# Attention and MLP in one kernel: weights cast in GpSimd's DMAs, two chunks of q, k, v asked for ahead of them, V copies ahead of loads, spare PSUM banks in the ramp

## The chip, the cores and the metric

One core of one Trainium2 chip. The metric is the device time of one execution in microseconds (us). Times are medians of a kernel's runs, all of them fast ones except where it is said (a run counts as slow when it is over 1.5% above the fastest of its kernel); "the profile" is one profiled execution. PE is TensorE, ACT is ScalarE, DVE is VectorE, POOL is GpSimd, SP is SyncE. Most DMAs of this kernel are issued from SP's queue (SPq).

## The reference, cut to what matters

```python
# q, k, v: (4, 8, 768, 64) fp32; heads 0, 2, 6 see all earlier keys ("retrieval"),
# the others see the first 4 keys (sinks) and a window of 64 ("stream")
scores = q @ k.T / 8, masked;  a = softmax(scores);  attn = a @ v
x = attn as (3072, 512)
h = x @ w_in                       # 512 x 2048
return maximum(0.01 * h, h) @ w_out   # 2048 x 512
```

## The kernel before

It works in 8 chunks of 384 tokens, two to a batch element. Per chunk it loads q, k, v (nine DMAs of 256 KB in rows of 256 B), casts them to bf16, transposes q and k on PE ("preparation"), runs attention, then the in-projection (16 steps of 4 matmuls) and the out-projection (3 tiles of 16 matmuls). From chunk 2 on these are interleaved; chunks 0 and 1 are the ramp.

`va` holds V. `vb` holds V shifted by 64 tokens and `vs` the sink rows; both are made from `va` by DMAs on SP's queue, "the V copies". They are wanted by the first stream head of an attention. Other names in the profile's lines: `kb` and `qb` are the bf16 casts of k and q, `kt` and `qt` their transposes, `ksink` the sink keys, `at` and `ats` the softmax weights, `po` and `xs` the output of attention, `pt` the PSUM tile of transposes, `psS` that of scores, `ph` and `py` those of the in- and the out-projection.

```python
def load_w(which, i):                     # 1 MB of fp32 weights into a staging tile
    t = rot.tile([128, 4, 512], FP32, name="wf", tag="wf", bufs=2)
    nc.sync.dma_start(out=t[:], in_=src)
# ... cast_w then casts it to bf16 with two copies on DVE and two on GpSimd

def cast_chunk(n):
    # ... cast k and q (chunk 0: DVE and ACT; else GpSimd)
    for g in range(3):
        nc.gpsimd.tensor_copy(va[i][:, 3 * c + g, :, 0:D], src[:, g])
    # ... V copies: vs (5 DMAs, first chunk of a batch element) and vb (2 DMAs), nc.sync

load(0, "kqv"); load_w("in", 0); load_w("in", 1)
cast_chunk(0)
for f in prep_slots(0) + attention_slots(0): f()
# ... 16 in-projection steps of chunk 0, with load(1) and weight loads and casts between them
load(2, "kqv")
cast_chunk(1)                             # its V copies stand behind load(2) on SP's queue
for f in prep_slots(1) + attention_slots(1): f()
# ... 16 in-projection steps of chunk 1
load(3, "kqv"); cast_chunk(2)
merge(out_slots(0), prep_slots(2) + attention_slots(2))
for n in range(2, NCH):
    load(n + 2, "kqv"); cast_chunk(n + 1)    # where they exist
    merge(weave(in_slots(n), out_slots(n - 1)), prep_slots(n + 1) + attention_slots(n + 1))
for f in out_slots(NCH - 1): f()
```

The softmax here doesn't subtract the row's maximum and nothing guards it: scores larger than these inputs give would overflow.

## Time and profile before

| | before |
|---|---|
| time, median (runs before the prediction) | 321.59 us |
| span of the profile | 319.7 us |
| ramp: start of the first out-projection matmul | 96.5 us |
| from there to the end of the span | 223.2 us |
| PE waiting for vb | 17.2 us in 5 waits |

The ramp's end is read off the time line of PE: the first matmul of the tile `py`. It cuts the span into a part where PE has holes and a part where PE is the bound. In a line of waits the three numbers are total us, how often, and the longest. In a time line they are start and length, then engine, line and operation, and in brackets how long the engine had stood idle and what ended it. The lines themselves are in the prediction.

### The profile page before, as it was taken

What the parts mean: (1) busy time and instruction counts of PE and PEld (TensorE: products, weight loads), DVE (VectorE), ACT (ScalarE), POOL (GpSimd) and SP (SyncE); (2) the same over time, 40 slices, a digit from 0 to 9 for tenths busy, and PEclk for the clock granted to TensorE, in tenths of its full rate; (3) what the DMA queues carried; (4) which work ended last, traced back from release to release, by engine and by line L of the source; (5) the groups of instructions that cost most, each with busy time, mean ns of one, the idle gap of its engine ahead of it and who ended that gap; (6) DMA issues with size and microseconds to landing.
All of it is one profiled execution on the core that took longest, in us unless ns stands there. A gap on an engine that the chain in (4) does not pass through costs nothing.

```text
span 319.7 us, 5340 instructions
## 1 busy us (share of the span) xinstructions
PE 257.2 (80%) x2107; PEld 149.8 (47%) x2136; DVE 119.4 (37%) x323; ACT 137.7 (43%) x296; POOL 60.5 (19%) x123
## 2 busy tenths in 40 slices
PE   0476974617897888999987989899969899999984
PEld 0244532315453444566554645565536456654431
DVE  4555524104325655243532453335334423311011
ACT  2144550507361442766262526673535357643300
POOL 6340254100074602400060024000510000000000
PEclk9996796758599999999997999999999999999999
DMA  9940799970399109900982089006920200000011
GB/s 172 282 137 3 254 229 318 221 146 1 136 281 156 57 35 202 209 35 2 194 141 69 30 172 232 10 35 138 192 67 35 83 36 20 16 35 33 33 66 66
DMA packets 84024, 36.56 MB, mean 114 GB/s; under 512 B 75808, under 2 KB 75808, under 8 KB 84000
## 3 DMA queue, kind: packets, MB, share of 16 engines
q1 hardware_dynamic: 84000, 36.24, 51.1%
q8 instruction: 16, 0.26, 0.4%
q14 instruction: 8, 0.07, 0.1%
HBM read 27.26 MB, written 6.29 MB: 105 GB/s over the span
## 4 chain that ended last, share of the span: by engine, by line
PE 47%; DMA 16%; DVE 13%; SPq 12%; issue 4%; POOL 4%; ACT 2%; POOLq 0%; ACTq 0%
PE py L364 18%; PE ph L350 11%; SPq L67 11%; DMA vb<-va 6%; PE po L198 5%; DMA qf<-in_q_dram 5%; DMA vf<-in_v_dram 4%; PE pt L165 3%; DVE kt L171 3%; DVE o L368 3%; PE psS L234 3%; PE pt L303 2%; DVE xs L297 2%; PE psS L269 2%; DMA wf<-in_moe_w_out_dram 2%
## 5 line engine op out<-in xcount | busy, mean ns | idle before, releaser
L350 PE MATMUL ph<-xt,w_in_bf 128*128 128x384 bf16 x512 | 106.0, 339 | 0.1
L364 PE MATMUL py<-w_out_bf,g 128*128 128x512 bf16 x355 | 97.0, 381 | 4.0 <-DVE o L368 2.3
L352 ACT ACTIVATE g<-ph 128x384 bf16<-128x384 f32 x128 | 63.0, 492 | 82.9 <-PE ph L350 82.4
L350 PEld LDWEIGHTS <-w_in_bf 128*128 128x128 bf16 x512 | 48.0, 101 | 33.5 <-issue 7.7
L239 ACT ACTIVATE at<-psS 128x384 bf16<-128x384 f32 x84 | 40.5, 492 | 23.0 <-PE psS L234 22.3
L364 PEld LDWEIGHTS <-g 128*128 128x128 bf16 x384 | 33.6, 98 | 27.7 <-issue 5.3
L243 DVE TENSOR_TENSOR at<-at,m_caus 128x128 bf16<-128x128 bf16 x72 | 17.4, 270 | 47.6 <-ACT at L239 47.6
L368 DVE COPY o<-py 128x512 f32<-128x512 f32 x24 | 16.6, 691 | 47.1 <-PE py L364 46.9
L171 DVE COPY kt<-pt 64x384 bf16<-64x384 bf16 x64 | 22.7, 355 | 20.4 <-PE pt L165 19.8
L234 PE MATMUL psS<-qt,kt 128*128 128x384 bf16 (+2 forms) x108 | 29.4, 315 | 0.8 <-ACT at_sink L214 0.4
L198 PE MATMUL po<-vb,ats 128*128 128x65 bf16 x100 | 11.9, 199 | 17.6 <-DMA vb<-va 17.2
L198 PE MATMUL po<-va,at 128*128 128x65 bf16 x252 | 23.5, 203 | 0.8 <-DVE at L243 0.6
L165 PE MATMUL pt<-ident,qb 128*128 128x128 bf16 x96 | 12.2, 239 | 14.4 <-DVE kt L171 11.0
L198 PEld LDWEIGHTS <-ats 128*128 128x128 bf16 x240 | 12.1, 102 | 22.8 <-issue 11.3
L304 ACT ACTIVATE xt<-pt 128x384 bf16<-128x384 bf16 x32 | 15.7, 490 | 15.9 <-PE pt L303 15.6
L165 PE MATMUL pt<-ident,kb 128*128 128x128 bf16 x96 | 12.0, 233 | 12.5 <-DVE kb L137 9.0
L198 PEld LDWEIGHTS <-at 128*128 128x128 bf16 x252 | 17.4, 104 | 8.0 <-DVE at L243 2.5
L278 DVE TENSOR_TENSOR ats<-ats,m_win 128x384 bf16<-128x384 bf16 x40 | 14.9, 372 | 16.3 <-ACT ats L274 16.1
L274 ACT ACTIVATE ats<-psS 128x384 bf16<-128x384 f32 x40 | 19.2, 490 | 3.9 <-PE psS L269 3.7
L141 POOL CAST kb<-kf 128x512 bf16<-128x512 f32 x21 | 12.4, 614 | 40.1 <-DMA kf<-in_k_dram 39.9
L297 DVE TENSOR_TENSOR xs<-po,linv 128x384 bf16<-128x384 f32 x32 | 17.8, 558 | 1.1
L165 PEld LDWEIGHTS <-qb 128*128 128x128 bf16 x96 | 6.4, 103 | 24.8 <-DVE kt L171 14.8
(45 smaller groups left out, 196.8 us busy)
## 6 DMA issues: line engine op xcount, KB each, us to landing
kf<-in_k_dram SPq DMA_DIRECT2D x24, 256.0 KB
qf<-in_q_dram SPq DMA_DIRECT2D x24, 256.0 KB
vf<-in_v_dram SPq DMA_DIRECT2D x24, 256.0 KB
out_dram<-o SPq DMA_DIRECT2D x24, 256.0 KB
wf<-in_moe_w_in_dram SPq DMA_DIRECT2D x4, 1024.0 KB
wf<-in_moe_w_out_dram SPq DMA_DIRECT2D x4, 1024.0 KB
vb<-va SPq DMA_DIRECT2D x8, 195.0 KB
vb<-va SPq DMA_DIRECT2D x8, 130.0 KB
```

Of the source, the lines that this page charges most:

```text
L67: nc.sync.dma_start(out=t[:, g], in_={"q": qr, "k": kr, "v": vr}[nm][b, c, :, :, g])
L165: nc.tensor.transpose(pt[:, g, :], tb[:, g, 2 * p : 2 * p + 2, :], ident[:])
L171: nc.vector.tensor_copy(kt[i][r, p, hh, CH * c : CH * c + CH], pt[r, 0:3, :])
L198: nc.tensor.matmul(o, lhsT=lhsT, rhs=rhs, start=first, stop=last, skip_group_check=True)
L234: nc.tensor.matmul(s[:, off : off + w], lhsT=kt[i][:, p, hh, 128 * kj : 128 * kj + 128], rhs=qt()[:, p, lo:CH], start=(j == 0), stop=(j == ...
L239: nc.scalar.activation(out=a[:, 0:off], in_=s[:, 0:off], func=ACTF.Exp, scale=SM)
L274: nc.scalar.activation(out=av_, in_=s[:, 0:CH].rearrange("p (j e f) -> p j e f", j=3, e=2), func=ACTF.Exp, scale=SM)
L297: nc.vector.tensor_tensor(xs[:], po[p][:, :, :, 0:D], linv.to_broadcast([128, 3, 2, D]), op=ALU.mult)
L350: nc.tensor.matmul(ph[:, 0:CH], lhsT=w_in_bf[:, g, 128 * t : 128 * t + 128], rhs=xts[n][:, g, :], start=(g == 0), stop=(g == KG - 1))
L352: nc.scalar.activation(out=gs[n][:, t, :], in_=ph[:, 0:CH], func=ACTF.Prelu, alpha=0.01)
L364: nc.tensor.matmul(py[n][:], lhsT=gs[n][:, ng, 128 * tt : 128 * tt + 128], rhs=w_out_bf[:, ng, :], start=(ng == 0), stop=(ng == NG - 1))
L368: nc.vector.tensor_copy(o[:], py[n][:])
```

## The change

Its intent: take the weights off SP's queue and their casts off DVE and GpSimd, so that they can be asked for early; have chunk 1's q, k, v in hand when chunk 0's attention ends; merge attention 1 with in-projection work; and issue a chunk's V copies before the next chunk's loads. The core of the diff:

```diff
     def load_w(which, i):
-        t = rot.tile([128, 4, 512], FP32, name="wf", tag="wf", bufs=2)
-        nc.sync.dma_start(out=t[:], in_=src)
+        if which == "in":
+            nc.gpsimd.dma_start(out=w_in_bf[:, :, c], in_=w_in_r[:, :, c])   # casts
+        else: # ... the same for w_out
     load(0, "kqv")
-    load_w("in", 0)
-    load_w("in", 1)
+    load(1, "kqv")
# ... chunk 0 only: transposes alternate between two banks, scores use ph's two banks too,
# ... half of the copies to kt go to ACT; the last two output tiles use ph's banks
-    cast_chunk(0)
-    for f in prep_slots(0) + attention_slots(0): f()
-    # ... casts and loads of weights, load(1), all of in_slots(0), load(2), cast_chunk(1)
+    cast_chunk(0, between=lambda: load_w("in", 0))
+    zeros(1)
+    for f in prep_slots(0) + attention_slots(0): f()
+    cast_chunk(1, between=lambda: [load_w("in", i) for i in (1, 2, 3)])
+    # ... load_w("out", 0..3); load(2, "kqv")
+    for f in ins0[0:4] + prep_slots(1): f()
+    merge(ins0[4:12], a1)
+    for f in ins1[0:12] + ins0[12:16] + ins1[12:16]: f()
+    cast_chunk(2)
     load(3, "kqv")
-    cast_chunk(2)
     for n in range(2, NCH):
+            cast_chunk(n + 1)
             load(n + 2, "kqv")
-            cast_chunk(n + 1)
```

`between` runs after the casts of k and q and before those of v. `ins0` and `ins1` are the 16 in-projection steps of chunks 0 and 1, `a1` is the attention of chunk 1, and `zeros(1)` clears the second set of buffers for k and v; before, it came after attention 0.

More of the change, by code (lines that the diff above doesn't have):

```diff
@@ L70, in load_w @@
     def load_w(which, i):
-        t = rot.tile([128, 4, 512], FP32, name="wf", tag="wf", bufs=2)
-        src = w_in_r[:, :, 512 * i : 512 * i + 512] if which == "in" else w_out_r[:, 4 * i : 4 * i + 4, :]
-        nc.sync.dma_start(out=t[:], in_=src)
-        stage[which, i] = t
+        if which == "in":
+            c = slice(512 * i, 512 * i + 512)
+            nc.gpsimd.dma_start(out=w_in_bf[:, :, c], in_=w_in_r[:, :, c])
+        else:
+            c = slice(4 * i, 4 * i + 4)
+            nc.gpsimd.dma_start(out=w_out_bf[:, c, :], in_=w_out_r[:, c, :])
     load(0, "kqv")
-    load_w("in", 0)
-    load_w("in", 1)
+    load(1, "kqv")
     ident = one.tile([128, 128], BF16, name="ident")
@@ L123, with pt_tile, cast_chunk @@
         nc.gpsimd.memset(a[:, :, 1:3, :], 0.0)
+    pt_n = [0]
+    def pt_tile(n):
+        pt_n[0] += 1
+        tag, bufs = ("py", 1) if n == 0 and pt_n[0] % 2 else ("pt", 1)
+        return ps.tile([128, 8, 128], BF16, name=tag, tag=tag, bufs=bufs)
     cast = {}
     qts = {}
-    def cast_chunk(n):
+    def cast_chunk(n, between=None):
         b, c = divmod(n, 2)
@@ L142, in cast_chunk @@
             cast[nm, n] = tb
+        if between:
+            between()
         src = stage["v", n]
@@ L161, in one_pair @@
         def one_pair(nm, p):
-            pt = ps.tile([128, 4, 128], BF16, name="pt", tag="pt", bufs=1)
+            pt = pt_tile(n)
             tb = cast[nm, n]
@@ L170, in one_pair @@
                 r = slice(64 * hh, 64 * hh + 64)
-                nc.vector.tensor_copy(kt[i][r, p, hh, CH * c : CH * c + CH], pt[r, 0:3, :])
+                if hh == 1 and n == 0:
+                    nc.scalar.activation(out=kt[i][r, p, hh, CH * c : CH * c + CH], in_=pt[r, 0:3, :], func=ACTF.Copy)
+                else:
+                    nc.vector.tensor_copy(kt[i][r, p, hh, CH * c : CH * c + CH], pt[r, 0:3, :])
                 h = 2 * p + hh
@@ L198, in av, with score @@
             nc.tensor.matmul(o, lhsT=lhsT, rhs=rhs, start=first, stop=last, skip_group_check=True)
-        def score(nm="ps"):
-            return ps.tile([128, 512], FP32, name="psS", tag="psS", bufs=2)
+        sc = [0]
+        def score():
+            sc[0] += 1
+            tag = "ph" if n == 0 and sc[0] % 2 else "psS"
+            return ps.tile([128, 512], FP32, name=tag, tag=tag, bufs=2)
         units = []
@@ L300, in x_t @@
         def x_t(p, xs):
-            pt = ps.tile([128, 4, 128], BF16, name="pt", tag="pt", bufs=1)
+            pt = pt_tile(n)
             for j in range(3):
@@ L354, in in_slots, with out_slots @@
         return [lambda t=t: tick(t) for t in range(NG)]
-    def out_slots(n):
+    def out_slots(n, tags=("py", "py", "py")):
         counts = [[3, 3, 3, 3, 4], [3, 3, 3, 3, 4], [3, 3, 3, 3, 2, 2]]
@@ L361, in part @@
             if lo == 0:
-                py[n] = ps.tile([128, 512], FP32, name="py", tag="py", bufs=1)
+                py[n] = ps.tile([128, 512], FP32, name=tags[tt], tag=tags[tt], bufs=1 if tags[tt] == "py" else 2)
             for ng in range(lo, hi):
@@ L377, in out_slots @@
         return slots
-    def cast_w(which, i):
-        t = stage[which, i]
-        for g in range(4):
-            dst = w_in_bf[:, g, 512 * i : 512 * i + 512] if which == "in" else w_out_bf[:, 4 * i + g, :]
-            if g < 2:
-                nc.vector.tensor_copy(dst, t[:, g, :])
-            else:
-                nc.gpsimd.tensor_copy(dst, t[:, g, :])
     def merge(ms, as_):
@@ L406, in weave @@
         return r
-    cast_chunk(0)
+    cast_chunk(0, between=lambda: load_w("in", 0))
+    zeros(1)
     for f in prep_slots(0) + attention_slots(0):
         f()
-    cast_w("in", 0)
-    load_w("in", 2)
-    zeros(1)
+    cast_chunk(1, between=lambda: [load_w("in", i) for i in (1, 2, 3)])
+    for i in range(4):
+        load_w("out", i)
+    load(2, "kqv")
     ins0 = in_slots(0)
-    def with_weights(t):
-        def f():
-            if t == 0:
-                cast_w("in", 1)
-                load_w("in", 3)
-            if t == 4:
-                load(1, "kqv")
-                cast_w("in", 2)
-                load_w("out", 0)
-            if t == 8:
-                cast_w("in", 3)
-                load_w("out", 1)
-            ins0[t]()
-        return f
-    for t in range(NG):
-        with_weights(t)()
-    load(2, "kqv")
-    cast_chunk(1)
-    for f in prep_slots(1) + attention_slots(1):
-        f()
+    for f in ins0[0:4] + prep_slots(1):
+        f()
+    a1 = attention_slots(1)
+    merge(ins0[4:12], a1)
     ins1 = in_slots(1)
-    for t in range(NG):
-        if t in (4, 8, 12):
-            cast_w("out", t // 4 - 1)
-            if t < 12:
-                load_w("out", t // 4 + 1)
-        ins1[t]()
-    cast_w("out", 3)
+    for f in ins1[0:12] + ins0[12:16] + ins1[12:16]:
+        f()
+    cast_chunk(2)
     load(3, "kqv")
-    cast_chunk(2)
     merge(out_slots(0), prep_slots(2) + attention_slots(2))
@@ L454 @@
         if n + 1 < NCH:
+            cast_chunk(n + 1)
             if n + 2 < NCH:
                 load(n + 2, "kqv")
-            cast_chunk(n + 1)
             a = prep_slots(n + 1) + attention_slots(n + 1)
         merge(weave(in_slots(n), out_slots(n - 1)), a)
-    for f in out_slots(NCH - 1):
+    for f in out_slots(NCH - 1, ("py", "ph", "ph")):
         f()
```

## The prediction

> **What bounds the kernel now.** I read the page's busy shares first, then the slices, then the waits of TensorE (PE), then the time lines of the stretches that those point to.
>
> ```profile
> span 319.7 us, 5340 instructions
> PE 257.2 (80%) x2107; PEld 149.8 (47%) x2136; DVE 119.4 (37%) x323; ACT 137.7 (43%) x296; POOL 60.5 (19%) x123
> PE   0476974617897888999987989899969899999984
> PEclk9996796758599999999997999999999999999999
> ```
>
> A slice is 8 us. From about 97 us on PE is near 9 tenths at full clock: there the kernel is bound by PE. Before that, in the ramp, PE has holes and the granted clock falls to 5 to 7 tenths. So the ramp is where time can be won, and the waits say what makes its holes:
>
> ```profile
> PE po L198 <- DMA vb<-va: 17.2, 5, 9.4
> PE pt L165 <- DVE kt L171: 11.0, 25, 0.9
> PE pt L303 <- DVE xs L297: 6.7, 10, 0.9
> PE pt L165 <- POOL qb L141: 2.9, 3, 1.0
> PE py L364 <- DVE o L368: 2.3, 3, 0.8
> ```
>
> (total us, times, longest.) The first is PE waiting for vb, the shifted copy of V. The time lines of SyncE's queue and of PE show why:
>
> ```profile
> 47.93 1.81 SPq L73 DMA_DIRECT2D wf<-in_moe_w_out_dram  x2
> 49.80 7.81 SPq L67 DMA_DIRECT2D kf<-in_k_dram  x3
> 57.70 3.86 SPq L67 DMA_DIRECT2D qf<-in_q_dram  x3
> 61.60 3.34 SPq L67 DMA_DIRECT2D vf<-in_v_dram  x3
> 65.04 1.09 SPq L153 DMA_DIRECT2D vb<-va  x1
> 66.23 0.54 SPq L154 DMA_DIRECT2D vb<-va  x1
> ...
> 70.47 0.21 PE L198 MATMUL po<-vb,ats 128*128 128x65 bf16 x1 [9.36 <-DMA vb<-va]
> ```
>
> Nine loads of the next chunk stand in the queue ahead of the two small copies that attention 1 needs, and PE stands still for 9.36 us. The cadence of the loads is seen in what GpSimd (POOL) waits for:
>
> ```profile
> 45.85 0.61 POOL L141 CAST qb<-qf 128x512 bf16<-128x512 f32 x1 [0.59 <-DMA qf<-in_q_dram]
> 47.05 0.62 POOL L141 CAST qb<-qf 128x512 bf16<-128x512 f32 x1 [0.59 <-DMA qf<-in_q_dram]
> 48.26 0.62 POOL L141 CAST qb<-qf 128x512 bf16<-128x512 f32 x1 [0.59 <-DMA qf<-in_q_dram]
> ```
>
> One 256 KB load lands each 1.2 us, about 218 GB/s. The two 1 MB weight chunks behind them are cast at 55.09 and 57.96 us, so 1 MB takes about 3 us. These two rates are my model of the DMA engines.
>
> **What the Trainium skill says.** "DMA: Bandwidth & Descriptors", section "SWDGE vs HWDGE vs iDMA": a cast during a DMA is only for GpSimd's queue, whose software writes the descriptors. The same page, "Issuing engines are not separate DMA queues": both queues run on the same 16 engines, so the new queue adds no bandwidth. Its "Queues, rings and completion order": an engine goes round its rings packet by packet, so a second queue shares instead of standing in line. The trace before has one data queue, so it can't confirm this; its 75808 packets under 512 B do say that the loads move in small packets, and a queue with 2 KB rows may take more than half of the engines. "TensorE: Matmul & The Clock Gate", Part 1: PE runs at half clock until some 3.4 us of sustained work. The trace agrees: weight loads of the first in-projection come 320 ns apart at 34 us and about 170 ns apart from 36.6 us on.
>
> **The change part by part.**
>
> Casts. 16 weight casts on DVE (8 at 515 and 8 at 526 ns) and 16 on POOL (725 ns) go: 8.3 and 11.6 us of busy time on engines that are 37% and 19% busy. Off the path nearly everywhere, worth about nothing by themselves. HBM bytes read stay the same. What counts is that the weights leave SyncE's queue and need no staging buffers, so all eight can be asked for early.
>
> Chunk 0's preparation. DVE's chain for a pair is 0.35 + 0.37 (kt) + 0.37 (qt) and two transposes, 2.25 us with one bank (first kt copies at 10.02, 12.33, 14.58, 16.84). With half of kt on ACT and two banks I expect 1.1 us per pair. But the compiled order now puts zeros(1), two 1.34 us memsets, on DVE before the first kt copy: start at 13.0 instead of 10.0. 13.0 + 4.5 = 17.5 us against 18.2 before. GpSimd then delays the sink keys: V casts, its own part of zeros(1) (1.5 us), five copies of 0.18 us, done at about 19.6. No gain here.
>
> Chunk 0's vb, the bad part. In the compiled order SyncE's queue has all nine loads of chunk 1 ahead of the V copies of chunk 0, and each transfer waits until the one eight places before it has landed (eight semaphores in turn). So the second vb copy waits for the 17th load. Before, v of chunk 0 was cast at 13.52, so nine loads took 10.8 us from 2.7. The 17th lands at 2.7 + 17 x 1.2 + 3 (w_in 0 shares the engines) = 26.1 us; the copy lands at about 30 with some contention from w_in 1 to 3, which POOL asks for at about 24.5. Attention 0 needs it 3.8 us after its start (18.1 to 21.9 before), now at about 23. So PE stands for about 7 us, on a path where before it did not wait (vb issued at 15.2 and 16.2, used at 21.9). The rest of attention 0 took 9.7 us and is about the same: end at 40 instead of 31.5 us.
>
> The rest of the ramp. First four in-projections: 16 matmuls, partly at half clock, 4.5 us. Preparation of chunk 1: eight slots at about 1.1 us on one bank, 8.7. Attention 1 merged with eight in-projections: attention 1 alone took 55.5 to 82.9 less the 9.4 wait, 18 us, with PE half empty; ACT has 25 + 8 activations of 0.49 us, 16.2 us, so the merged stretch is 18. The other 20 in-projections: 80 matmuls at 0.165, 13.2 us. Sum 40 + 4.5 + 8.7 + 18 + 13.2 = 84.4 us, where the out-projection of chunk 0 starts; before it was 96.5. Gain 12.1 us. Of the casts of chunk 1 and the weights I expect no wait here: 7 MB of weights at 3 us and nine loads of chunk 2 from 26 us on are done by about 62 us.
>
> Later iterations. V copies ahead of loads takes the remaining vb waits, 17.2 - 9.4 = 7.8 us, and the clock dip that follows one of them (slice 24 at 7 tenths): 0.3 of 8 us at most, I take 1.6.
>
> Tail. Two of the three waits for the eviction of py (2.3 in 3) go with ph banks: 1.6 us.
>
> Sum: 12.1 + 7.8 + 1.6 + 1.6 = 23.1 us of 321.6, so 298.5; I say 298.
>
> **The rivals.** First, no wait for vb in chunk 0: then attention 0 ends at 32 and the time is about 290. For it speaks only that the author meant the copies to go ahead; against it the compiled order. Second, the weights flood the engines: if 2 KB packets take turns with 256 B packets, the HBM loads crawl for as long as weights are queued, 9 us for w_in 1 to 3. If POOL asks for these before the 17th load has landed, vb of chunk 0 comes at about 35 and the time is 303 to 306. Against it: POOL's casts of chunk 1's q come first in its order and wait for loads of about 24 us. Third, DMAs with a cast are slow, or their descriptors block POOL for long. At half the rate 7 MB would take 42 us and be done at about 80, still before the out-projection at 84; only slower than that would it bound the ramp, at 310 or more. No profile line speaks to it yet. Fourth, a gain hidden anyway: from 97 us PE is the bound, and 12 us of ramp can't be hidden by it, since nothing in the steady part waits for anything but PE and vb.
>
> **Range and chances.** The mean of these, weighed, stays at 298. Low 289 (no chunk 0 wait, or a warmer ramp), high 307 (flood). Even the bad rivals stay under 315, which is 2%: faster 0.96, same 0.03, slower 0.01.
>
> **What would show it.** Right: one wait of PE for vb of some 7 us at about 23 to 30 us, and none later; first out-projection at about 84 us; loop iterations at about 30 us instead of 32 to 33; one eviction wait in the tail; POOL without weight casts. Wrong: no wait there; PE waiting for w_in or w_out; a new wait for ksink; granted clock still low from 40 to 70 us, which would lengthen the merged stretch beyond 18 us.

## The result, and the profile after

The changed kernel takes 305.1 us (302.66 to 305.24, 4 runs), before 321.25 (4 runs): ratio 0.947, 95% interval 0.942 to 0.953. A ratio is the mean time of one kernel's fast runs over that of the other's of the same rounds, so it isn't quite the ratio of the medians. The time lies inside the predicted range, 7 us above the predicted value.

The page of the changed kernel, busy shares and slices:

```profile
span 303.3 us, 5335 instructions
PE 250.4 (83%) x2136; PEld 146.6 (48%) x2136; DVE 110.7 (36%) x303; ACT 138.4 (46%) x300; POOL 56.2 (19%) x115
PE   0260366687897898999999989999999899999994
PEclk9999977589999999999999999999999999999998
```

The steady part is now 9 nearly throughout and its clock holds until the last slice. But the hole of before has not gone from the ramp: it has moved to slices 3 and 4 (counted from 0), about 22 to 35 us, where PE before had 6 and 9 tenths. The waits of PE name it:

```profile
PE po L213 <- DMA vb<-va: 12.4, 1, 12.4
PE pt L177 <- DVE kt L186: 8.8, 23, 0.9
PE pt L322 <- DVE xs L316: 4.1, 6, 0.9
PE ph L230 <- POOL ksink L189: 1.2, 1, 1.2
PE py L383 <- DVE o L387: 0.8, 1, 0.8
```

Five waits for vb of 17.2 us have become one of 12.4. SP's queue and PE around it:

```profile
12.51 3.60 SPq L67 DMA_DIRECT2D kf<-in_k_dram  x3
16.16 3.47 SPq L67 DMA_DIRECT2D qf<-in_q_dram  x3
19.68 3.59 SPq L67 DMA_DIRECT2D vf<-in_v_dram  x3
23.38 3.25 SPq L161 DMA_DIRECT2D vs<-va  x5
26.73 0.53 SPq L162 DMA_DIRECT2D vb<-va  x1
27.36 0.57 SPq L163 DMA_DIRECT2D vb<-va  x1
...
34.99 0.21 PE L213 MATMUL po<-vb,ats 128*128 128x65 bf16 x1 [12.45 <-DMA vb<-va]
```

The V casts that the copies read ended at 17.2 us. Yet the copies are issued at 26.7 and 27.4, behind nine loads of chunk 1 which the new order puts first. That is the same fault as before, one chunk earlier. And then they take 7.6 us to land, as the chain of work has it (start and length):

```profile
27.36 7.59 DMA vb<-va
```

The two parts of the span: the ramp ends at 92.4 us instead of 96.5, and the rest takes 210.9 instead of 223.2. So of the 16.4 us that the span lost, 4.1 come from the ramp and 12.3 from the part after it, though most of the change's lines are about the ramp.

### The profile page after: what moved, and what is told of

Its sections match the earlier page's. It is cut to its first block, busy times and chain, and to the rows that moved or that the text cites. A ratio compares the mean times of both kernels' runs of the same rounds, so it can differ in the third digit from the quotient of the medians.

```text
span 303.3 us, 5335 instructions
## 1 busy us (share of the span) xinstructions
PE 250.4 (83%) x2136; PEld 146.6 (48%) x2136; DVE 110.7 (36%) x303; ACT 138.4 (46%) x300; POOL 56.2 (19%) x115
## 4 chain that ended last, share of the span: by engine, by line
PE 71%; DVE 12%; SPq 6%; DMA 4%; ACT 3%; issue 2%; POOL 1%; ACTq 0%; DVEq 0%
PE ph L369 25%; PE py L383 23%; PE po L213 6%; SPq L67 6%; DVE kt L186 5%; PE pt L177 5%; PE psS L253 4%; DMA vb<-va 3%; PE pt L322 2%; PE ph L383 2%; DVE o L387 2%; DMA qf<-in_q_dram 2%; DVE xs L316 2%; PE psS L288 2%; PE psS L230 1%
## 5 line engine op out<-in xcount | busy, mean ns | idle before, releaser
L369 PE MATMUL ph<-xt,w_in_bf 128*128 128x384 bf16 x512 | 104.6, 334 | 0.0
L383 PE MATMUL py<-w_out_bf,g 128*128 128x512 bf16 x352 | 94.3, 379 | 1.1 <-DVE o L387 0.8
L258 ACT ACTIVATE at<-psS 128x384 bf16<-128x384 f32 x81 | 39.1, 491 | 9.9 <-PE psS L253 9.7
L262 DVE TENSOR_TENSOR at<-at,m_caus 128x128 bf16<-128x128 bf16 x72 | 16.1, 251 | 49.9 <-ACT at L258 49.9
L186 DVE COPY kt<-pt 64x384 bf16<-64x384 bf16 x56 | 19.9, 355 | 31.6 <-PE pt L177 31.1
L387 DVE COPY o<-py 128x512 f32<-128x512 f32 x22 | 15.2, 690 | 39.5 <-PE py L383 39.3
L253 PE MATMUL psS<-qt,kt 128*128 128x384 bf16 (+2 forms) x103 | 27.7, 307 | 1.0 <-ACT ats L293 0.6
L213 PE MATMUL po<-va,at 128*128 128x65 bf16 x252 | 22.5, 198 | 1.5 <-DVE at L262 1.4
L213 PE MATMUL po<-vb,ats 128*128 128x65 bf16 x100 | 11.7, 197 | 12.6 <-DMA vb<-va 12.4
L297 DVE TENSOR_TENSOR ats<-ats,m_win 128x384 bf16<-128x384 bf16 x40 | 16.5, 413 | 14.8 <-ACT ats L293 14.3
L213 PEld LDWEIGHTS <-ats 128*128 128x128 bf16 x240 | 11.8, 100 | 17.9 <-DMA vb<-va 11.8
L323 ACT ACTIVATE xt<-pt 128x384 bf16<-128x384 bf16 x30 | 14.7, 489 | 10.5 <-PE pt L322 10.3
L177 PEld LDWEIGHTS <-kb 128*128 128x128 bf16 x96 | 8.6, 103 | 21.8 <-DVE kb L147 9.5
L189 POOL COPY ksink<-kt 64x4 bf16<-64x4 bf16 x20 | 3.6, 186 | 81.9 <-DVE kt L186 81.8
```

What stands on the lines that cost most here:

```text
L177: nc.tensor.transpose(pt[:, g, :], tb[:, g, 2 * p : 2 * p + 2, :], ident[:])
L186: nc.vector.tensor_copy(kt[i][r, p, hh, CH * c : CH * c + CH], pt[r, 0:3, :])
L213: nc.tensor.matmul(o, lhsT=lhsT, rhs=rhs, start=first, stop=last, skip_group_check=True)
L253: nc.tensor.matmul(s[:, off : off + w], lhsT=kt[i][:, p, hh, 128 * kj : 128 * kj + 128], rhs=qt()[:, p, lo:CH], start=(j == 0), stop=(j == ...
L258: nc.scalar.activation(out=a[:, 0:off], in_=s[:, 0:off], func=ACTF.Exp, scale=SM)
L369: nc.tensor.matmul(ph[:, 0:CH], lhsT=w_in_bf[:, g, 128 * t : 128 * t + 128], rhs=xts[n][:, g, :], start=(g == 0), stop=(g == KG - 1))
```

## The experiments

All results were correct. In a second group the kernel before measured 322.07 us (7 runs), in a third 321.26 (7 runs, one of them slow), so the ratios to before are comparable. The end of the ramp and the length of the rest are of each run's own profile.

| kernel | time us | ratio to before | ramp ends | rest |
|---|---|---|---|---|
| before | 321.25 | 1 | 96.5 | 223.2 |
| the change | 305.1 | 0.947 | 92.4 | 210.9 |
| e1_vfirst | 292.2 | 0.909 | 79.6 | 210.9 |
| e2_wlate | 300.3 | 0.934 | 89.3 | 211.0 |
| e3_zeroslate | 303.9 | 0.946 | 90.9 | 210.8 |
| b1_copies_first | 300.7 | 0.936 | 85.3 | 212.7 |
| e4_vz (three fast runs; its profile is of the slow one) | 291.0 | 0.908 | 82.4 | 210.9 |
| e5_nobanks | 293.6 | 0.913 | 81.9 | 210.9 |
| e6_vzw | 294.65 | 0.915 | 80.9 | 210.9 |
| e7_merge | 286.8 | 0.892 | 72.7 | 210.9 |

### Is it the place of the copies in the queue? (e1_vfirst)

```diff
-    load(1, "kqv")
+    load(1, "k")
-    cast_chunk(0, between=lambda: load_w("in", 0))
+    cast_chunk(0, between=lambda: load_w("in", 0))
+    load(1, "qv")
```

> The changed kernel with one thing moved: the V copies of chunk 0 go into SyncE's queue behind k of chunk 1 only, ahead of its q and v. My theory (the 12.4 us wait for vb is made by the place of the copies in that queue, the weights only lengthen it): the copies are issued at about 18 us and land at about 21 to 23, the wait of PE for vb in chunk 0 falls from 12.4 to under 2 us, all that follows moves forward by 9 to 12 us, time about 293 to 296 (ratio to the changed kernel 0.965). Rival (the wait is hidden anyway behind the loads of chunk 1 and the weights, which the next stages need): the wait vanishes, but PE then waits as long for casts of chunk 1 or for w_in, time within 3 us of 305.

292.2 us, a little under the 293 to 296 expected. SP's queue and PE:

```profile
16.76 3.25 SPq L161 DMA_DIRECT2D vs<-va  x5
20.11 0.53 SPq L162 DMA_DIRECT2D vb<-va  x1
20.74 0.53 SPq L163 DMA_DIRECT2D vb<-va  x1
21.32 1.94 SPq L67 DMA_DIRECT2D qf<-in_q_dram  x3
...
23.05 0.24 PE L213 MATMUL po<-vb,ats 128*128 128x65 bf16 x1
```

The matmul has no bracket: PE didn't wait for vb at all. Its first use of vb came 11.9 us sooner (23.05 instead of 34.99), the ramp ends 12.8 us sooner, and the rest is as long as in the changed kernel. So the wait was not hidden behind anything: its length was on the path that sets the end. Moving six loads (q and v of chunk 1) behind seven copies (five of 0.5 KB, two of 195 and 130 KB) is worth 12.9 us, where the whole change had brought 16.2.

### What do the weights add to the wait? (e2_wlate)

```diff
-    cast_chunk(1, between=lambda: [load_w("in", i) for i in (1, 2, 3)])
+    cast_chunk(1)
+    for i in (1, 2, 3): load_w("in", i)
```

> The changed kernel with w_in chunks 1 to 3 asked for after the V casts of chunk 1 instead of before, about 3 us later. Flood theory (2 KB rows of the weights take turns with 256 B rows on the engines, so the copies, issued at 26.7 and 27.4, land only at about 35): the copies land at about 30, the wait for vb falls from 12.4 to 7 or 8 us, time about 300. Rival (the copies are late only because their issue waits for the 17th load): wait and time unchanged, 12.4 us and 305.

300.3 us, and the wait for vb is 9.2 us. The copies were issued at 26.70 and 27.32, as in the changed kernel; only their way to SBUF was shorter (chain of work, then PE):

```profile
27.32 3.96 DMA vb<-va
...
31.32 0.21 PE L213 MATMUL po<-vb,ats 128*128 128x65 bf16 x1 [9.24 <-DMA vb<-va]
```

7.59 against 3.96 us, with the same issue times, and w_in 1 to 3 asked for at 27.2 instead of 24.3 us. So the weights did hold up the copies, by 3.6 us, and the rival, that only the place in the queue counts, falls. The 9.2 us of wait that stay come with that place, as e1_vfirst shows; how much of them is still due to the weights, which were now asked for just when the copies were issued, is not separated.

### Do the memsets at the start cost anything? (e3_zeroslate)

```diff
-    zeros(1)
     for f in prep_slots(0) + attention_slots(0): f()
...
+    zeros(1)
     cast_chunk(2)
```

> The changed kernel with zeros(1), two 1.34 us memsets on DVE and three on GpSimd, moved to just before the casts of chunk 2. Preparation of chunk 0 then starts at about 10.2 instead of 13.0 us. My theory: hidden, since attention 0 waits for vb until 35 us in any case: the wait grows by what the start gains, time unchanged within 1 us of 305. Rival (the start of the ramp sets the end): time 302.

303.9 us (303.5 to 305.24), which is within the noise of 305.1. The profile says where the start's gain went: PE reached its first use of vb at about 20.6 instead of 22.5 us, and then waited 13.0 us instead of 12.4. So the wait took 0.6 us of the 1.9 that the start gained. The other 1.3 came through, because in this run the copies landed sooner (first use of vb at 33.67 instead of 34.99). The loads had come sooner too: the last V cast of chunk 0 began at 15.86 instead of 16.61. It began at 16.09 in e2_wlate, where the memsets stood as in the changed kernel, so this looks like chance; then the start's gain was hidden, as expected.

### The order of the copies alone, on the kernel before (b1_copies_first)

```diff
-    load(2, "kqv")
     cast_chunk(1)
+    load(2, "kqv")
# ... the same swap for load(3) / cast_chunk(2) and for load(n + 2) / cast_chunk(n + 1)
```

> The kernel before with one part of the change alone: each chunk's V copies ahead of the next loads in SyncE's queue (three swaps), weights, buffers and banks as before. My theory: this part carries the gain; all five waits for vb, 17.2 us, go, and with the clock dips behind them the time is about 302 to 305, so no slower than the whole change. Rival (the weights on GpSimd's queue carry it, and the waits for vb only turn into waits for loads that now come later): 315 to 320.

300.7 us (300.33 to 301.74): this part alone is not only no slower than the whole change, it is 4.4 us faster (ratios to before 0.936 and 0.947, from two groups; their 95% intervals, 0.929 to 0.943 and 0.942 to 0.953, just touch, and no run of the one lies among those of the other). No wait of PE for vb is left in its profile. SP's queue at the place where PE had stood for 9.36 us:

```profile
48.65 1.81 SPq L73 DMA_DIRECT2D wf<-in_moe_w_out_dram  x2
52.10 0.48 SPq L153 DMA_DIRECT2D vb<-va  x1
53.15 0.47 SPq L154 DMA_DIRECT2D vb<-va  x1
53.67 6.84 SPq L67 DMA_DIRECT2D kf<-in_k_dram  x3
```

The copies now stand ahead of the loads. The rest after the ramp takes 212.7 us against 223.2, so the later swaps give 10.5 us; the swap in the ramp gives 11.2 (96.5 to 85.3). The other 1.8 us of the rest (212.7 to 210.9) lie in the last three output tiles, where the change gives two of them banks of their own: from the first matmul of these tiles to the end of the span it is 16.5 us here (281.52 to 298.0) and 14.4 in the changed kernel (288.86 to 303.3).

### Combining: four more kernels

The first (e4_vz) takes e1_vfirst and e3_zeroslate together:

> The changed kernel with the V copies of chunk 0 early (as in e1_vfirst, 292.2 us) and zeros(1) late (as in e3_zeroslate, which gained nothing alone). If zeros(1) was only hidden behind the wait for vb, it must now show: preparation of chunk 0 starts 3 us earlier, but the V copies are issued no earlier than the V casts allow (about 17 to 21 us), so I expect 1 to 2 us of the 3: about 290.5 to 291.5. If it costs nothing at all: 292.

Its four runs are 290.88, 290.98, 294.02 and 295.24 us; the last, the profiled one, counts as slow, and the median of the others is 291.0 (292.5 of all four). Beside e1_vfirst's 292.2 a gain of about 1 us is possible, and not shown. Its profile, of the slow run, has PE waiting 2.8 us for the sink keys, which GpSimd makes after the V casts, and 1.6 us for vb. The fast profile of e7_merge below, which starts in the same way, has 1.4 and 1.2. So with the long wait for vb out of the way, what is left at the start hangs on when V is loaded and cast.

The second (e5_nobanks) takes the spare banks back from it (transposes on one bank, all copies to kt on DVE, scores on two banks):

> e4_vz with the spare banks of the ramp taken back: one bank for the transposes of chunk 0, all of kt copied by DVE, two banks for its scores. If the banks do what they are for, preparation of chunk 0 takes 9 us instead of 5.5 and attention 0 somewhat longer: 2 to 3.5 us slower than e4_vz. Rival (attention 0 is a chain of PE, ACT and DVE, and the V copies bound its start): within 1 us of e4_vz.

293.6 us (292.88 to 294.55). Ratios to before are 0.913 here and 0.908 with the banks, some 1.7 us apart, with intervals that overlap (0.907 to 0.920 and 0.899 to 0.917). And the profiled run had a start of its own: the last q load was cast at 13.61 instead of 10.26 us, while w_in 0, asked for at about 6 us, was under way. The next kernel, which has the banks, had the same late q load (13.62). It reached its first in-projection at 32.36 us, this one at 35.40, so the banks may bring some 3 us by then. Of these 1.0 is left at the end of the ramp (80.9 and 81.9). With one profile of each, what the spare banks bring to the time stays open.

The third (e6_vzw) asks for w_in 1 to 3 later, on top of e4_vz:

> e4_vz with w_in chunks 1 to 3 asked for after the V casts of chunk 1, which gave 4 to 5 us to the changed kernel (e2_wlate). If that gain was only the flood in front of chunk 0's V copies, it is now nothing: within 1 us of e4_vz. If late weights help the loads in other ways: 2 us or more faster; if w_in now comes too late: slower, with PE waiting for w_in.

294.65 us (292.2 to 294.97), not faster. So with chunk 0's copies out of the way, late weights bring nothing that shows, which fits a flood that only mattered ahead of those copies. PE has no wait for w_in either. In its profile, too, the last q load came late (PE waits 3.0 us for its cast). What made it slower than e4_vz is not shown.

The fourth (e7_merge) goes on from there, and changes what fills the preparation of chunk 1:

```diff
-    for f in ins0[0:4] + prep_slots(1): f()
+    merge(ins0[0:8], prep_slots(1))
-    merge(ins0[4:12], a1)
+    merge(ins0[8:14], a1)
# ... ins0[14:16] follow later instead of ins0[12:16]
```

> e6_vzw with eight in-projections of chunk 0 merged into the preparation of chunk 1 and six into attention 1, instead of four ahead of it and eight. In the changed kernel that preparation left PE idle for about 5 of its 8 us at half clock. I expect 3 to 5 us less than e6_vzw, about 286 to 288, the fastest of all; rival: w_in chunk 1 lands too late for it, PE waits for w_in, no gain.

286.8 us (286.11 to 288.07): the fastest of all, 0.892 of before, 7.9 us under e6_vzw and 4.2 under the fast runs of e4_vz, where 3 to 5 were expected. Which of the two is nearer to what the merge is worth is open. In the profiles the late q load of e6_vzw plays no part in it: attention 0 was done at nearly the same time in both (the next stage starts at 32.36 us there and at 32.68 here), and the 8.2 us of ramp are gained after that. Four in-projections and the preparation of chunk 1 took 12.9 us in e6_vzw, the preparation with eight in 8.9 here; attention 1 took 21.0 there and 17.9 here, with two steps less in it; the in-projections that follow took 14.7 and 13.3.

The stretches show a second effect beside the filled holes. e6_vzw (after each engine's busy us and count come granted clock, DMA share and GB/s):

```profile
30.00:40.00 10.00, 7.30 (x42) 4.01 (x42) 2.45 (x8) 2.95 (x6) 8.18 (x13) 0.66 0.80 138
40.00:50.00 10.00, 6.74 (x33) 3.56 (x34) 2.89 (x9) 2.27 (x6) 0.61 (x1) 0.53 1.22 196
50.00:60.00 10.00, 8.68 (x114) 5.75 (x113) 4.31 (x14) 7.61 (x18) 1.23 (x2) 0.96 1.22 207
```

and this one over the same time:

```profile
30.00:60.00 30.00, 23.69 (x246) 15.07 (x244) 12.03 (x37) 17.80 (x40) 9.71 (x16) 1.00 1.14 191
```

The 1.00 is not to be taken at its word for the start of a run. There the view shows 1.00, while three transposes take 0.48 to 0.53 us, as long as later at a granted clock of 0.50. By their length PE ran at half rate here until about 35 us, and at full rate from then on; in e6_vzw it fell back to half during the preparation. First e6_vzw, then this kernel:

```profile
39.33 0.33 PE L177 MATMUL pt<-ident,kb 128*128 128x128 bf16 x3 [0.45 <-DVE qt L179]
40.47 0.47 PE L177 MATMUL pt<-ident,qb 128*128 128x128 bf16 x3 [0.82 <-DVE kt L186]
...
34.23 0.52 PE L177 MATMUL pt<-ident,qb 128*128 128x128 bf16 x3
35.60 0.33 PE L177 MATMUL pt<-ident,kb 128*128 128x128 bf16 x3
40.71 0.34 PE L177 MATMUL pt<-ident,qb 128*128 128x128 bf16 x3 [0.17 <-DVE kt L186]
```

So with transposes alone and a copy between each (24 matmuls in 7.9 us), the clock fell, and with in-projections between them (56 in 8.9 us) it did not. This agrees with the Trainium skill, "TensorE: Matmul & The Clock Gate", Part 1, by which PE's clock follows how busy PE has been of late. How much of the gain is clock and how much filled holes is not separated here.

## Why the prediction was right or wrong

**Right: the wait in chunk 0.** The prediction read it off the compiled order: a second wait for vb, on a path that had none, because nine loads stand ahead of the copies and the second copy waits for the 17th load. The copies were issued at 26.7 and 27.4 us, predicted from 24.9 to 26.1 on; PE stopped at 22.5, predicted about 23. The place in the queue is shown by e1_vfirst; the wait for the 17th load is not seen in the traces. In e2_wlate, with the same issue times, that load had landed when its cast began at 25.73 us, and the copy was issued at 27.32. What the queue shows in between is its own pace: the loads some 1.2 us apart until about 23 us, then the five copies to vs and the first to vb 0.6 to 0.7 us apart. The first rival (no such wait, 290) was what e1_vfirst then made of the kernel, at 292.2.

**The term that was mis-sized: the landing of the copies.** "The copy lands at about 30": it landed at 35.0, and the wait was 12.4 us, not 7. That is the second rival, the flood, which the prediction had put at 35 and then weighed down because POOL's casts of chunk 1's q come first. They did come first, but ended at 24.3 us, so w_in 1 to 3 were asked for about 3 us before the copies were issued. The prediction's own numbers had met the condition that it set for this rival: w_in asked for at 24.5 us, before the 17th load at 26.1. The rival's time, 303 to 306, is the one that was measured, so the result lies inside the range only by the part of it that was kept for the flood. e2_wlate shows the flood's share, 3.6 us of landing.

**Other terms of the ramp.** After the copies had landed, attention 0 took 9.0 us (predicted 10); four in-projections 5.0 (4.5); preparation of chunk 1 7.8 (8.7); the merged attention 1 20.8 (18); the last in-projections 14.7 (13.2). With the landing, 5.0 late, that sums to 5.0 - 1.0 + 0.5 - 0.9 + 2.8 + 1.5 = 7.9 us, and the ramp did end at 92.4, not 84.4. The merged stretch is the one to learn from: the prediction named its fear of a low clock, and the clock was 0.62 between 50 and 60 us and 0.87 between 60 and 70 (the stretch runs from 56.9 to 77.7). That this made its 2.8 us is an argument, not a run. At the same mean clock over that stretch (0.86 here, 0.88 and 0.87 there) e1_vfirst and e6_vzw took 20.8 and 21.0 for it. In e7_merge, with the clock up and two steps less in it, it took 17.9. Two steps are 8 matmuls 0.175 us apart (84 in 14.7 us), 1.4 us; so by an estimate about 1.5 of the 2.9 us between them are the clock's. Of the prediction's signs of being wrong two came: the low clock, and a new wait for ksink, of 1.2 us.

**Chunk 0's preparation.** "I expect 1.1 us per pair": it was 1.44 (kt copies of DVE at 12.98, 14.35, 15.79, 17.22). In the trace ACT's half of kt starts only when DVE's half has ended (13.30 after 12.98 + 0.29), so the two halves did not run side by side. "No gain here" was right, and e3_zeroslate shows that this start was hidden.

**Later iterations and tail.** Predicted 7.8 + 1.6 for the waits and the clock dip; b1_copies_first, which changes only the order, shortened the rest by 10.5. Tail predicted 1.6; it was about 2 (16.5 to 14.4), and the waits for the eviction of py went from 2.3 in 3 to 0.8 in 1, as said. Together 12.3 against 11.0.

**The casts.** "Worth about nothing by themselves" is consistent with the runs, but the prediction did not say what b1_copies_first shows: that the whole gain of the change could be had from its order of copies, and that its other ramp parts first had to pay for a wait of their own making. Only with that wait removed do they bring something: e1_vfirst is 8.5 us under b1_copies_first in time and 7.5 in the profiles' spans, 5.7 of these in the ramp. No run separates the weights on GpSimd's queue, the earlier loads and the merge from each other, so which of them brings the 5.7 us stays open.

**The third rival,** slow casting DMAs, fell: no wait of PE for w_in or w_out is in the profile of the change.

## What to carry to other kernels

Read each queue in program order and ask of every transfer that an engine waits for: how many loads stand ahead of it, and what does its issue wait for? Here prefetching further brought such a wait to a place that had none, and a gain in the steady part can hide that a change has lost in the ramp, so split the span and judge each part by itself. And where preparation leaves PE nearly idle, put dense matmuls between its steps: here they filled the holes, and the clock stayed up.

## What the Trainium skill lacked or had wrong

- "DMA: Bandwidth & Descriptors", "Queues, rings and completion order", says that an engine goes round its rings packet by packet. It has no figure for what that does to small rows beside large ones. Here loads in 256 B rows, which landed 1.2 us apart in the kernel before, were cast at 43.52, 50.00 and 53.52 us while weights in 2 KB rows were queued on the other queue, as GpSimd's time line of the changed kernel shows:

```profile
43.52 0.62 POOL L151 CAST kb<-kf 128x512 bf16<-128x512 f32 x1 [12.42 <-DMA kf<-in_k_dram]
50.00 0.62 POOL L151 CAST kb<-kf 128x512 bf16<-128x512 f32 x1 [5.87 <-DMA kf<-in_k_dram]
53.52 0.62 POOL L151 CAST kb<-kf 128x512 bf16<-128x512 f32 x1 [2.90 <-DMA kf<-in_k_dram]
```

- The same page, "Anatomy of one DMA", calls the making of descriptors "small, variable" and has no figure for how long an issue holds GpSimd's queue. Here the issue of one casting DMA of 1 MB held GpSimd's queue for 0.74 to 0.89 us, three in a row for 2.2 us.
- The same page gives no rate for a DMA with a cast. Here the four of w_out took 15.0 to 22.4 us from issue to landing, queued one behind the other and beside other loads; no run here measures one alone.
